# A written order for the experts' phase: 889 named steps in one list, in place of loops and a planner

## Chip, cores and metric

One core of one Trainium2 chip. The time is device microseconds (us) of one execution. A core has a matrix engine (PE, TensorE), three engines for elementwise work (DVE is VectorE, ACT is ScalarE, POOL is GpSimd), and SP (SyncE), which here only issues transfers (DMAs). Each engine takes its instructions in the order in which the program has them for that engine, and waits at an instruction until what it needs is there. So what a kernel decides, beside the work itself, is five orders.

## What is computed

The reference chains three layers. The first is attention with a window of 128 positions, the second a gated layer with a spatial mix; the change touches neither. The third, which the code calls the experts' part, is this:

```python
B, S, D = x.shape            # 4, 576, 512
E, Hd, K = 4, 64, 2          # experts, head size, experts kept for a position
logits = x @ w_gate
topk = np.argpartition(-logits, K, axis=-1)[..., :K]
w = softmax(logits[topk])
for e in range(E):
    q, k, v = x @ wq[e], x @ wk[e], x @ wv[e]
    scores = scale * (q @ k.transpose(0, 2, 1))
    scores = np.where(causal, -1e9, scores)
    a = softmax(scores)
    ye = a @ v @ wo[e]
    out += (gate of e at the position, 0 if e is not kept) * ye
```

The four experts are four heads of causal attention. Their gates are folded into the softmax's row factors, so that the four outputs add up in one product with `wo`.

## The kernel before

**Tiling.** A batch `b` (0 to 3) has 576 positions: four tiles of 128 queries (`j` = 0 to 3) and one of 64 (`j` = 4, in which two heads share the 128 rows). A tile sees the keys up to its own last position, so tile 0 has 128 keys a row and tile 3 has 512. Products of 32-bit data are made in three passes (`PASSES`): high by high, high by low, low by high part; a result in PSUM is therefore always taken in two steps, the high part by ACT (a copy), the low part by DVE (a subtraction, `lo_part`).

**The steps of a batch.** `load_g` fetches the batch's input from DRAM (`g_dram`) and splits it. `proj` makes queries and keys: 8 banks of 12 matmuls (tile `pq`: pair of heads, query or key, half of the positions), then the values (`values`, tile `pvB`, 12 matmuls each) and the gates (`gates`, 14 small operations on DVE, POOL and ACT). For each tile `scores_b` makes the scores of both pairs of heads (`psB`); `row_items` subtracts the row's maximum (DVE, one fused operation that also reduces) and takes the exponential (ACT); `weigh` makes the row factors (DVE) and scales (POOL). The weights must then be turned round for the next product. DVE turns blocks of 32 by 32 in place, and SP writes the tile to DRAM (`mid`, four DMAs) and reads it back in another order (`pTB`): `cross_items` and `read_back`. The last three tiles (`y, a, z`) are turned on PE instead (`turn_b`, tile `ptB`). `attend_b` multiplies by the values (`pxB`), `take_b` takes the result (`o`), `out_tile` multiplies by `wo` (`pout`), copies (`ot`) and stores.

**Buffers.** Four PSUM banks (`D`) serve `pq`, `pvB`, `pxB` and `pout` in turn; two double banks (`S`) serve `psB` and `ptB`. There are three buffers for a tile's weights (`pB`), three for the turned ones (`pTB`), three in DRAM (`mid`), two for a batch's queries, keys and values. A tile's DVE operation on the scores (L1168) therefore waits until the write of the tile three before it has landed.

**What sets the order.** Two ways are in use. The attention and gated layers follow long written lists of named steps (`OPENING`, `FIRST`, `SECOND`). The experts' phase does not: a loop over the 20 tiles places the PE's work, with `pull` interleaving projections and outputs between the scores and `attend_b` of a tile four places back (`LAG`), and the class `Flow` places the other engines' work from costs in ns written beside each operation (`item`) and from the PE time that it counts along. An operation goes to its engine's program when, by these costs, the PE has come that far:

```python
def pump(self):
    ...
    engine, ns, op, after, ok = items[0]
    at = max(chain[2], self.free.get(engine, 0.0))
    if at > self.pe or (ok and not ok()):
        break
```

A tile's write and read stand in one chain, with a pause between them that is taken from a table by `j`; a projection's 12 matmuls, or an output's 6, go into one bank, and the next bank is begun when they are done.

Of the kernel before, what the change touches and what calls it, by code (L numbers as in the profile page):

```python
# [10 lines left out]
F32 = mybir.dt.float32  # L11
# [12 lines left out]
P = 128  # L24
DM = 512
# [158 lines left out]
class Flow:  # L184


    def __init__(self):
        self.pe = 0.0
        self.free = {}
        self.chains = []  # L190
        self.count = 0

    def add(self, items, rank=1, delay=0.0, then=None):
        self.count += 1
        chain = [rank, self.count, self.pe + delay, deque(items), then]
        self.chains.append(chain)
        self.chains.sort(key=lambda c: c[:2])
        return chain

    def pump(self):  # L200
        moved = True
        while moved:
            moved = False
            for chain in list(self.chains):
                items = chain[3]
                while items:
                    engine, ns, op, after, ok = items[0]
                    at = max(chain[2], self.free.get(engine, 0.0))
                    if at > self.pe or (ok and not ok()):
                        break  # L210
                    items.popleft()
                    op()
                    self.free[engine] = at + ns
                    chain[2] = at + ns + after
                    moved = True
                if not items and chain in self.chains:
                    self.chains.remove(chain)
                    if chain[4]:
                        chain[4](chain[2])
                    moved = True  # L220
                    break

    def coming(self):
        return min((max(c[2], self.free.get(c[3][0][0], 0.0)) for c in self.chains if c[3] and (not c[3][0][4] or c[3][0][4]())), default=1e12)

    def work(self, ns):
        end = self.pe + ns
        self.pump()
        while (at := self.coming()) <= end:
            self.pe = max(self.pe, at)  # L230
            self.pump()
        self.pe = end

    def until(self, done):
        self.pump()
        while not done():
            self.pe = max(self.pe, self.coming())
            self.pump()

    def finish(self, chain):  # L240
        self.until(lambda: chain not in self.chains)


def item(engine, ns, op, after=0.0, ok=None):
    return engine, ns, op, after, ok
# [3 lines left out]
def block_kernel(ctx, tc, qP, kP, v, w_in, wspT, bsp, w_outT, wcat, wo, relt, tri, out):  # L249
# [683 lines left out]
    both = []  # L933

    def load_g(b, pool):
        G = x if b % 2 == 0 else x2
        f = pool.tile([P, 4, S], F32, tag="gf", name=f"gf{b}", bufs=1)

        def fetch(k, after=0.0):
            return "SP", 400.0, lambda: nc.sync.dma_start(f[:, k, :], g_dram[b, k]), after, None  # L940

        def parts():
            first = 2 if b > 1 else 4
            for k in range(first):
                yield fetch(k, 6000.0 if k == first - 1 else 0.0)
            for k in range(4):
                yield "ACT", 670.0, lambda k=k: nc.scalar.copy(G[0][:, k, :S], f[:, k, :]), 0.0, None
                on, ns, engine = ("DVE", 850.0, nc.vector) if b < 2 else ("POOL", 1430.0, nc.gpsimd)
                yield on, ns, lambda k=k, engine=engine: lo_part(G[1][:, k, :S], f[:, k, :], G[0][:, k, :S], engine), 2000.0 if b > 1 and 0 < k < 3 else 0.0, None
                if k + first < 4:  # L950
                    yield fetch(k + first)
            c = slice(64 * (b % 2), 64 * (b % 2) + 64)

            def high():
                if b % 2 == 0:
                    both[:] = [gfp.tile([P, 4, P], F32R, tag=f"both{i}", name=f"both{b}_{i}") for i in range(2)]
                nc.scalar.copy(both[0][:, :, c], f[:, :, 0:64])

            yield "ACT", 400.0, high, 0.0, lambda: tails_done[0] >= b // 2
            yield "POOL", 740.0, lambda: lo_part(both[1][:, :, c], f[:, :, 0:64], both[0][:, :, c], nc.gpsimd), 0.0, None  # L960

        return G, list(parts())

    tails_done = [0]
    G, gparts = load_g(0, gfp)
    for part in gparts:
        part[2]()
# [17 lines left out]
    QS, KS, QT, VS, GATE = {}, {}, {}, {}, {}  # L985

    flow = Flow()
    banks = []

    def bank(name):  # L990
        if len(banks) >= 4:
            flow.finish(banks[-4])
        banks.append(None)
        return len(banks) - 1, psD.tile([P, 512], F32, tag="D", name=name)

    def leave(n, *items, delay=250.0):
        banks[n] = flow.add(items, rank=0, delay=delay)
        return banks[n]

    gating = []  # L1000

    def gates(b, t0, n, after=()):
        if len(gating) > 1:
            flow.finish(gating[-2])
        vt = VS[b]
        lg = vt[:, t0 : t0 + n, 256:260]
# [24 lines left out]
        gating.append(flow.add([item(e, 230.0, op) for e, op in steps] + list(after)))
        gated[b, t0] = gating[-1]

    gated = {}

    def tail_gate(b):
        gt, gq = GATE[b]
        for o in range(2):
            yield item("ACT", 200.0, lambda o=o: nc.scalar.copy(gq[64 * o : 64 * o + 64, :], gt[0:64, 4, :].rearrange("p (r o) -> p o r", o=2)[:, o, :]))

    def values(b, t, stationary):
        at, pv = bank(f"pvB{b}_{t}")
        n = 0
        for i, j in PASSES:
            for k in range(4):
                nc.tensor.matmul(pv[:, :260], stationary(i, k), W[j][1][:, k, 512 - CUT :], start=(n == 0), stop=(n == 11))  # L1046
                n += 1
            if n < 12:
                yield 4 * 120.0
        if t < 4:  # L1050
            vt = VS[b]
            leave(at, item("ACT", 370.0, lambda: nc.scalar.copy(vt[:, t, :], pv[:, :260])))
        else:
            leave(at, *(item("ACT", 370.0, lambda o=o, vt=VS[b - 1 + o]: nc.scalar.copy(vt[:64, 4, :], pv[64 * o : 64 * o + 64, :260])) for o in range(2)))
        yield 4 * 120.0
        return at

    def proj(b, G):

        GATE[b] = wk.tile([P, 5, E], F32, tag="gt", name=f"gt{b}"), wk.tile([P, 2], F32, tag="gq", name=f"gq{b}")  # L1060
# [5 lines left out]
        for pr in range(2):  # L1066
            for role in (1, 0):
                hl = [t[:, pr, :] for t in (KS[b] if role else QS[b])]
                c0 = role * 256 + pr * 128
                for s in range(2):  # L1070
# [3 lines left out]
                    for i, j in PASSES:  # L1074
# [3 lines left out]
                        if n < 12:  # L1078
                            yield 4 * 133.0
# [22 lines left out]
        for chain in projected[b]:  # L1102
            flow.finish(chain)
# [399 lines left out]
```

## Time and profile before

| | us |
|---|---|
| median of 3 runs (450.99 to 451.58) | 451.36 |
| the profiled execution, its own time | 454.39 |
| its span, first to last instruction | 452.3 |
| PE busy in the span | 425.8 |
| DVE, ACT, POOL busy | 308.7, 239.2, 150.5 |
| PE's first matmul of the experts' phase | 268.03 |
| its last one starts at 447.52 and ends at about | 449.2 |

The rows further down come from the profiled execution; times in them count from the span's start. A busy PE is not PE at its best: matmuls overlap, their ends are modelled, and a matmul at half clock is busy for longer. Time in which an engine other than PE idles costs nothing by itself.

### The profile page before, as it was taken

Reading aid. Unit: us, or ns where it says so; the run is one execution under the profiler, and the core shown is the slowest. Engines: PE = TensorE matmul, PEld = TensorE weight load, DVE = VectorE, ACT = ScalarE, POOL = GpSimd, SP = SyncE. Lnnn points to the kernel's source line nnn. Section 1 sums busy time; section 2 is a strip of 40 time slices with the busy share of each in tenths; the row PEclk is TensorE's granted clock in tenths of the full one; section 3 lists DMA queues with packets and bytes.
Section 4 is the critical chain, followed back from the end, with each engine's and each line's share of the span. In section 5 each row is a group of like instructions: output and inputs, shape, how many; then the busy total and the mean of one; then the engine's idle time right before and its main releaser. Section 6 shows DMA issues by size and latency. Waiting matters only on the chain.

```text
span 452.3 us, 11412 instructions
## 1 busy us (share of the span) xinstructions
PE 425.8 (94%) x4055; PEld 378.4 (84%) x4055; DVE 308.7 (68%) x1062; ACT 239.2 (53%) x746; POOL 150.5 (33%) x281
## 2 busy tenths in 40 slices
PE   7888999999999999999999999999968989999786
PEld 6566799899898989899989999989957978887564
DVE  5999999989988656872464235377765675776331
ACT  6977879644645544551351134467454444564541
POOL 2064433263344520443000002357644442341200
PEclk9999999999999999999999999999998999999899
DMA  8986674687947644234674200136976575697863
GB/s 260 337 313 238 173 219 123 209 276 219 270 144 234 171 112 120 63 77 128 210 280 157 100 1 0 54 93 170 268 217 190 150 182 171 170 207 239 205 232 94
DMA packets 76940, 80.01 MB, mean 177 GB/s; under 512 B 18002, under 2 KB 52946, under 8 KB 76500
## 3 DMA queue, kind: packets, MB, share of 16 engines
q1 hardware_dynamic: 76740, 79.15, 59.2%
q8 instruction: 32, 0.52, 0.5%
q14 instruction: 24, 0.20, 0.2%
q10 hardware_dynamic: 144, 0.13, 0.1%
HBM read 49.64 MB, written 29.62 MB: 175 GB/s over the span
## 4 chain that ended last, share of the span: by engine, by line
PE 61%; DMA 15%; DVE 15%; SPq 3%; ACT 2%; issue 2%; POOL 2%; DVEq 0%; POOLq 0%; ACTq 0%
PE pg L763 12%; PE pu L748 11%; PE pv L685 9%; DMA pTB<-mid 8%; DMA mid<-pB 6%; PE pq L1076 6%; PE px L659 5%; PE pw L915 4%; DVE pB L1216 3%; PE pxB L1288 3%; SPq L1218 3%; PE pvB L1046 2%; PE pg L766 2%; DVE p L298 2%; POOL pB L311 1%
## 5 line engine op out<-in xcount | busy, mean ns | idle before, releaser
L299 ACT ACTIVATE p<-p,st 128x128 f32<-128x128 f32 x144 | 56.3, 394 | 12.1 <-DVE st L298 6.7
L763 PE MATMUL pg<-wsp,vn 128*128 128x288 f32 x384 | 60.2, 296 | 1.0 <-ACT vn L720 1.0
L748 PE MATMUL pu<-x,win 128*128 128x288 f32 x384 | 57.5, 296 | 0.0
L763 PEld LDWEIGHTS pg<-wsp,vn 128*128 128x128 f32 x384 | 54.3, 188 | 3.3 <-ACT vn L720 1.2
L685 PE MATMUL pv<-win,x 128*128 128x512 f32 x216 | 56.1, 398 | 0.0
L1076 PE MATMUL pq<-x,W 128*128 128x288 f32 x384 | 55.0, 301 | 0.0
L748 PEld LDWEIGHTS pu<-x,win 128*128 128x128 f32 x384 | 53.4, 188 | 1.8 <-issue 0.9
L1076 PEld LDWEIGHTS pq<-x,W 128*128 128x128 f32 x384 | 52.1, 191 | 1.9 <-issue 1.5
L311 POOL TENSOR_SCALAR pB<-pB,stB 128x384 f32<-128x384 f32 (+4 forms) x64 | 35.8, 575 | 36.4 <-DVE stB L1192 27.6
L578 POOL TENSOR_TENSOR p<-p,st 128x512 f32<-128x512 f32 (+1 forms) x28 | 29.6, 1058 | 55.0 <-ACT p L299 24.6
L685 PEld LDWEIGHTS pv<-win,x 128*128 128x128 f32 x216 | 38.6, 188 | 8.0 <-issue 1.1
L1169 ACT ACTIVATE pB<-pB,stB 128x128 f32<-128x128 f32 (+3 forms) x64 | 35.8, 560 | 15.3 <-DVE stB L1168 13.7
L1288 PE MATMUL pxB<-pTB,vt 128*64 128x128 f32 (+2 forms) x480 | 28.9, 266 | 8.8 <-DMA pTB<-mid 8.7
L1288 PEld LDWEIGHTS pxB<-pTB,vt 128*64 128x64 f32 (+1 forms) x480 | 23.6, 140 | 14.0 <-DMA pTB<-mid 5.7
L1216 DVE STREAM_TRANSPOSE pB<-pB 128x1024 f32<-128x1024 f32 (+3 forms) x28 | 27.0, 984 | 9.4 <-POOL pB L311 9.2
L1168 DVE CUSTOM_DVE_ANT_0 pB<-psB,trit 128x128 f32<-128x128 f32 (+3 forms) x64 | 28.5, 480 | 5.4 <-DMA mid<-pB 5.2
L298 DVE CUSTOM_DVE_ANT_0 p<-ps,relm 128x128 f32<-128x128 f32 x128 | 30.1, 284 | 0.3
L613 POOL TENSOR_SCALAR_AFFINE_SELECT pU<-pT 128x512 f32<-128x512 f32 (+1 forms) x26 | 15.8, 619 | 38.5 <-DMA pT<-carry 37.8
L1330 PE MATMUL pout<-wo,o 128*128 128x512 f32 x102 | 27.3, 412 | 0.8 <-ACT o L1301 0.8
L771 DVE TENSOR_TENSOR g<-u,pg 128x288 f32<-128x288 f32 x32 | 14.4, 450 | 19.7 <-PE pg L766 19.5
L299 ACT ACTIVATION_READ_ACCUMULATOR p<-p,st 128x1 f32 x144 | 27.3, 190 | 0.0
L659 PE MATMUL px<-pU,v 128*64 128x128 f32 (+1 forms) x256 | 23.6, 266 | 1.4 <-DVE st L575 1.1
(183 smaller groups left out, 897.1 us busy)
## 6 DMA issues: line engine op xcount, KB each, us to landing
carry<-p SPq DMA_DIRECT2D x96, 64.0 KB, 2.0
pT<-carry SPq DMA_DIRECT2D x24, 256.0 KB, 2.9
q<-in_qP SPq DMA_DIRECT2D x20, 256.0 KB, 3.6
g_dram<-g SPq DMA_DIRECT2D x16, 288.0 KB, 2.9
gf<-g_dram SPq DMA_DIRECT2D x16, 288.0 KB, 5.6
raw<-in_w_in SPq DMA_DIRECT2D x8, 512.0 KB, 5.9
v<-in_v SPq DMA_DIRECT2D x16, 256.0 KB, 5.3
mid<-pB SPq DMA_DIRECT2D x16, 256.0 KB, 4.8
```

The source lines that it names most:

```text
L298: lambda: nc.vector.tensor_tensor_reduce(s_view, ps_view, tab, -0.125, FLT_MAX, ALU.add, ALU.min, nm),
L299: lambda: nc.scalar.activation(s_view, s_view, AF.Exp, bias=nm, scale=-1.0, accum_out=sm),
L311: nc.gpsimd.tensor_scalar(p, p, r, 0.0, op0=ALU.mult, op1=ALU.add)
L578: ops["m"] = lambda: nc.gpsimd.tensor_tensor(blocks, blocks, sm.unsqueeze(1).unsqueeze(3).to_broadcast([P, 4, n, 32]), op=ALU.mult)
L659: nc.tensor.matmul(px[64 * o : 64 * o + 64, hp, :qn], V_[b, t][:, h * 64 : h * 64 + 64], rhs, start=(t == max(0, j - 1)), stop=(t == j))
L685: nc.tensor.matmul(pv, x[i][:, k, t0 : t0 + P], win[j][:, k, 512:1024], start=(n == 0 and k == 0), stop=(n == 2 and k == 3))
L748: nc.tensor.matmul(pu[:, :HALF], win[i][:, k, m * P : (m + 1) * P], x[j][:, k, c], start=(n == 0 and k == 0), stop=(n == 2 and k == 3))
L763: nc.tensor.matmul(pg[:, :HALF], vn[i][k][:, m * P : (m + 1) * P], wsp[j][:, k, c], start=(n == 0 and k == 0), stop=False)
L1076: nc.tensor.matmul(pq[:, :HALF], W[i][c0 // CUT][:, k, c0 % CUT : c0 % CUT + P], G[j][:, k, c], start=(n == 0), stop=(n == 11))
L1169: item("ACT", 480.0 + 0.84 * kn, lambda: nc.scalar.activation(part(p, i), part(p, i), AF.Exp, bias=nm, scale=-1.0, accum_out=sm)),
L1216: items.append(item("DVE", 130.0 + 1.12 * (c1 - c0), lambda flat=flat: nc.vector.transpose(flat, flat)))
L1288: nc.tensor.matmul(px[64 * o : 64 * o + 64, pr, :qn], vt[:kb, c, (2 * pr + o) * 64 : (2 * pr + o) * 64 + 64], rhs(pr, c, o), start=(c == 0 ...
```

## The change

The loop, the class `Flow`, `item`, and the costs go. In their place stands `THIRD`, one list of 889 names, each of them one step; `act` looks a name up and issues its instructions. All five engines' programs follow from that one list. The matmuls are the same ones, 1,482 of them in the phase, and so are the operations of the other engines; their places differ.

Names: `L`, `GH`, `GL`, `BH`, `BL` load and split an input; `Q` is a third of a projection bank (4 matmuls), `qh` and `ql` take it; `V`, `vr` the same for values; `g` one of the gate's 14 operations; `S` the scores of one pair of heads; `l`, `e`, `f`, `m`, `T` the row operations of a tile; `w` its four writes, `R` its read; `A` its product with the values, `oh` and `ol` take it; `O` a third of an output (2 matmuls), `oc` copies, `o` stores; `t`, `c` turn a tile on PE.

```diff
-class Flow:
...
+THIRD = """
+    L1.0 L1.1 L1.2 L1.3 Q0.1.0.1.0 VZ0 VZ1 Z0 Q0.0.0.0.0 Z1 Q0.0.0.0.1 Q0.1.0.1.1 Q0.1.0.1.2 Q0.0.0.0.2 V0.2.0 qh0.1.0.1 qh0.0.0.0 V0.0.0 ql0.1.0.1
...
+    m3.0.1 m3.0.2 m3.0.3 A2.4 oh3.3 R3.4 ol3.3 O3.3.0 oh2.4 O3.2.0 ol2.4 O3.1.0 O3.3.1 O3.1.1 O3.3.2 O3.2.1 oc3.3 O3.2.2 O3.1.2 o3.3 oc3.2 t3.0.0
...
+TURNED = ((3, 2), (3, 1), (3, 0))
...
+    def project(b, pr, role, s, n):
+        pq = bank("pq", b, pr, role, s)
+        G, c0, c = inputs(b), role * 256 + pr * 128, slice(s * HALF, (s + 1) * HALF)
+        i, j = PASSES[n]
+        for k in range(4):
+            nc.tensor.matmul(pq[:, :HALF], W[i][c0 // CUT][:, k, c0 % CUT : c0 % CUT + P], G[j][:, k, c], start=(n == k == 0), stop=(n == 2 and k == 3))
...
+    def scores_b(b, j, pr):
+        q0, kn = TOK[j][0], keys_seen(j)
+        Q, K = heads(b, 0), heads(b, 1)
+        view = score_bank(b, j, pr)
...
+    def send(b, j):
+        p = weights(b, j)[0]
+        n, w, e = sizes(j)
+        mid = get(("mid", b, j), lambda: dram.tile([16 if j < 4 else 18, 32, 4, w], F32, tag=f"mid{w}", name=f"mid{b}_{j}", bufs=3))
+        for q in range(4):
             nc.sync.dma_start(mid[:n, :, q, :].rearrange("k i w -> i k w"), p[32 * q : 32 * q + 32, : n * w].rearrange("i (k w) -> i k w", w=w))
...
+    def out_tile(b, t, n, h=None):
+        c = slice(0, DM) if h is None else slice(256 * h, 256 * h + 256)
+        po = bank("pout", b, t, h)
+        o2 = made["o", b if t < 4 else b - 1, t]
+        i, j = PASSES[n]
+        for pr in range(2):
+            nc.tensor.matmul(po[:, : c.stop - c.start], o2[i][:, pr, :], wos[j][:, pr, c], start=(n == pr == 0), stop=(n == 2 and pr == 1))
...
+        else:
+            {"Q": project, "sp": spread, "V": value, "vr": value_take, "h": tail_gate, "S": scores_b, "l": row_min, "e": row_exp, "f": factors, "m": scale, "T": turn_blocks,
+             "w": send, "R": read_back, "t": turn_b, "c": turn_take, "A": attend_b, "oc": out_take, "o": out_store}[kind](*key)
...
-    todo = deque([proj(0, G)])
-    credit = [0.0]
...
-    for s in range(len(tiles) - 1):
-        b, j = tiles[s]
...
-        scores_b(*tiles[s])
-        due = tiles[s - LAG] if s >= LAG else None
-        for i in range(5):
-            if due and (state[due]["read"] or i == 2):
-                close_tile(due)
-                due = None
-            pull((5500.0 if s < 1 else RATE if s < 15 else 4600.0 if s < 18 else 2000.0) / 5)
...
+    for name in THIRD.split():
+        act(name)
```

**SP, around the writes of tiles (0, 3) and (0, 4).** `mid0_3` is the DRAM copy of tile (0, 3), `pTB0_3` its read, `gf3` a load of batch 3's input. Before:

```order
L1218 DMA mid0_3_4423<-pB0_3_4305 32x16x128 x4
L1218 DMA mid0_4_4495<-pB0_4_4394 32x18x64 x4
L1235 DMA pTB0_3_4666<-mid0_3_4423 128x4x512
L940 DMA gf3_4508<-g_dram_84 128x576
L1218 DMA mid1_0_4641<-pB1_0_4510 32x4x128 x4
L940 DMA gf3_4508<-g_dram_84 128x576
L1235 DMA pTB1_0_4756<-mid1_0_4641 128x512
L1235 DMA pTB0_4_4760<-mid0_4_4495 128x4x256
L1235 DMA pTB0_4_4760<-mid0_4_4495 64x256
```

And now:

```order
L1146 DMA mid0_4_4529<-pB0_4_4323 32x18x64 x4
L1146 DMA mid0_3_4575<-pB0_3_4373 32x16x128 x4
L930 DMA gf3_4419<-g_dram_84 128x576
L1156 DMA pTB0_4_4653<-mid0_4_4529 128x4x256
L1156 DMA pTB0_4_4653<-mid0_4_4529 64x256
L1146 DMA mid1_0_4716<-pB1_0_4495 32x4x128 x4
L1156 DMA pTB0_3_4752<-mid0_3_4575 128x4x512
L930 DMA gf3_4419<-g_dram_84 128x576
```

Tile (0, 4) is now written before (0, 3), and its read stands ahead of the write of (1, 0) where it stood behind that write and the read that waits for it.

**PE, around the product of tile (0, 3) with its values** (`pxB0_3`; `psB1_3` are scores of batch 1, `pq2` and `pq3` projections of batches 2 and 3, `pvB2` values of batch 2). Before:

```order
L1076 MATMUL pq2_1_1_1_4763<-x0_104,W0_388_3383 128x288 x4
L1076 MATMUL pq2_1_1_1_4763<-x1_105,W0_388_3383 128x288 x4
L1076 MATMUL pq2_1_1_1_4763<-x0_104,W1_388_3385 128x288 x4
L1288 MATMUL pxB0_3_4781<-pTB0_3_4666,vt0_3969 64x128 x16
L1076 MATMUL pq2_1_0_0_4810<-x0_104,W0_384_3382 128x288 x4
L1076 MATMUL pq2_1_0_0_4810<-x1_105,W0_384_3382 128x288 x4
L1076 MATMUL pq2_1_0_0_4810<-x0_104,W1_384_3384 128x288 x4
L1076 MATMUL pq2_1_0_1_4830<-x0_104,W0_384_3382 128x288 x4
```

And now:

```order
L1083 MATMUL psB1_3_1_4856<-k1_0_4103,q1_0_4088 128x512 x2
L1083 MATMUL psB1_3_1_4856<-k1_1_4104,q1_0_4088 128x512 x2
L1083 MATMUL psB1_3_1_4856<-k1_0_4103,q1_1_4089 128x512 x2
L1192 MATMUL pxB0_4_4868<-pTB0_4_4653,vt0_3834 64x64 x20
L1192 MATMUL pxB0_3_4892<-pTB0_3_4752,vt0_3834 64x128 x16
L1025 MATMUL pvB2_0_4918<-W0_388_3383,x0_104 128x260 x4
L1025 MATMUL pvB2_0_4918<-W1_388_3385,x0_104 128x260 x4
L1025 MATMUL pvB2_1_4945<-W0_388_3383,x0_104 128x260 x4
L1025 MATMUL pvB2_1_4945<-W1_388_3385,x0_104 128x260 x4
L1001 MATMUL pq3_0_0_1_4957<-x20_3811,W0_384_3382 128x288 x4
```

The product of (0, 3) now stands behind all projections of batch 2, all scores of batch 1 and the product of (0, 4), where it stood ahead of the last two.

**PE, the end** (`pout3_3` is the output of tile (3, 3), `ptB3_0` the turning of tile (3, 0)). Before:

```order
L1260 MATMUL ptB3_0_0_6055<-ident_74,pB3_0_5962 128x128 x4
L1330 MATMUL pout3_3_6061<-wo0_3801,o3_3_0_6048 128x512 x2
L1330 MATMUL pout3_3_6061<-wo1_3802,o3_3_0_6048 128x512 x2
L1330 MATMUL pout3_3_6061<-wo0_3801,o3_3_1_6049 128x512 x2
L1288 MATMUL pxB3_1_6071<-pTB3_1_0_6004,vt3_5410 64x128 x8
L1330 MATMUL pout3_1_6085<-wo0_3801,o3_1_0_6080 128x512 x2
L1330 MATMUL pout3_1_6085<-wo1_3802,o3_1_0_6080 128x512 x2
L1330 MATMUL pout3_1_6085<-wo0_3801,o3_1_1_6081 128x512 x2
L1288 MATMUL pxB3_4_6094<-pTB3_4_5919,vt3_5410 64x64 x20
L1330 MATMUL pout3_4_6118<-wo0_3801,o2_4_0_5907 128x512 x2
```

And now:

```order
L1192 MATMUL pxB2_4_6026<-pTB2_4_5786,vt2_4931 64x64 x20
L1210 MATMUL pout3_3_None_6054<-wo0_3801,o3_3_0_6047 128x512 x2
L1210 MATMUL pout3_2_None_6060<-wo0_3801,o3_2_0_5994 128x512 x2
L1210 MATMUL pout3_1_None_6064<-wo0_3801,o3_1_0_6018 128x512 x2
L1210 MATMUL pout3_3_None_6054<-wo1_3802,o3_3_0_6047 128x512 x2
L1210 MATMUL pout3_1_None_6064<-wo1_3802,o3_1_0_6018 128x512 x2
L1210 MATMUL pout3_3_None_6054<-wo0_3801,o3_3_1_6048 128x512 x2
L1210 MATMUL pout3_2_None_6060<-wo1_3802,o3_2_0_5994 128x512 x2
L1210 MATMUL pout3_2_None_6060<-wo0_3801,o3_2_1_5995 128x512 x2
L1210 MATMUL pout3_1_None_6064<-wo0_3801,o3_1_1_6019 128x512 x2
L1171 MATMUL ptB3_0_0_6084<-ident_74,pB3_0_5931 128x128 x4
L1192 MATMUL pxB3_4_6092<-pTB3_4_6050,vt3_5394 64x64 x20
```

Products stood alternating with the output that needs them; now three outputs are mixed in thirds and stand between the products of (2, 4) and (3, 4). In the order of SP, the read of (3, 4) is issued at `R3.4`, ahead of these nine thirds.

## Rows read from the trace of the kernel before

**Rows 1.** Windows: busy us of each engine by stage, clock, DMA share

```profile
core 0: us, PE busy (x) PEld busy (x) DVE busy (x) ACT busy (x) POOL busy (x), PEclk, DMA share, GB/s
60.00:220.00 160.00, 160.00 (x1691) 145.62 (x1684) 125.09 (x442) 82.80 (x287) 60.39 (x86) 1.00 0.56 164
...
268.00:300.00 32.00, 32.00 (x258) 31.07 (x257) 16.57 (x53) 15.98 (x45) 8.93 (x27) 1.00 0.16 44
...
328.00:345.00 17.00, 11.54 (x126) 9.47 (x124) 9.32 (x30) 7.92 (x25) 9.70 (x19) 0.97 0.72 209
...
268.00:449.30 181.30, 166.84 (x1483) 147.47 (x1481) 107.64 (x374) 91.48 (x270) 66.47 (x147) 0.98 0.60 163
449.30:452.30 3.00, 0.00 (x0) 0.00 (x0) 0.00 (x0) 0.35 (x1) 0.00 (x0) 1.00 0.34 102
```

**Rows 2.** Waits of PE from 268 us on: total, times, longest

```profile
PE pxB L1288 <- DMA pTB<-mid: 8.7, 6, 3.1
PE ptB L1260 <- DVE stB L1168: 2.7, 1, 2.7
PE pout L1330 <- ACT o L1301: 0.8, 2, 0.5
...
PE pout L1320 <- ACT o L1301: 0.5, 1, 0.5
```

**Rows 3.** Timeline of PE; brackets: idle before, and what ended it

```profile
303.61 1.66 PE L1138 MATMUL psB<-k,q 64*128 64x512 f32 x12
...
335.56 1.97 PE L1288 MATMUL pxB<-pTB,vt 128*64 128x128 f32 x32 [3.05 <-DMA pTB<-mid]
...
343.06 2.39 PE L1288 MATMUL pxB<-pTB,vt 128*64 128x64 f32 x40 [1.61 <-DMA pTB<-mid]
...
397.42 4.42 PE L1330 MATMUL pout<-wo,o 128*128 128x512 f32 x18
...
426.50 1.12 PE L1260 MATMUL ptB<-ident,pB 128*128 128x128 f32 x4 [2.69 <-DVE stB L1168]
```

**Rows 4.** Timeline of SP around the first long waits of PE

```profile
318.93 8.51 SPq L1218 DMA_DIRECT2D mid<-pB  x8
327.62 0.77 SPq L1235 DMA_DIRECT2D pTB<-mid  x1
...
337.16 1.92 SPq L1235 DMA_DIRECT2D pTB<-mid  x3
```

**Rows 5.** Windows of ten us: clock and transfers

```profile
320.00:330.00 10.00, 9.20 (x89) 8.29 (x87) 7.27 (x31) 5.52 (x21) 5.68 (x10) 1.00 0.99 255
...
340.00:350.00 10.00, 8.38 (x82) 7.43 (x81) 5.80 (x16) 3.64 (x11) 5.42 (x11) 0.83 0.69 191
...
420.00:430.00 10.00, 7.31 (x74) 5.72 (x72) 4.19 (x20) 4.75 (x15) 2.27 (x4) 0.83 0.87 194
```

**Rows 6.** Chain that ended last, in order of time: start, us, what

```profile
248.46 0.53 PE pg L763 x4
...
268.03 12.69 PE pq L1076 x96
280.72 5.74 PE pvB L1046 x48
...
294.21 3.88 PE pq L1076 x28
...
337.60 5.42 DMA pTB<-mid
...
376.10 4.11 DMA pTB<-mid
```

**Rows 7.** Waits of DVE from 268 us on

```profile
DVE pB L1168 <- DMA mid<-pB: 5.2, 2, 3.8
```

**Rows 8.** Window from the first read to the last ones

```profile
297.00:436.00 139.00, 125.94 (x1131) 110.04 (x1131) 90.86 (x322) 73.77 (x223) 57.74 (x121) 0.98 0.73 195
```

More of the change, by code (lines that the diff above doesn't have):

```diff
@@ L181, in drain @@
         self.credit = 0.0
-class Flow:
[L187 to L241, printed above, removed]
@@ L248, in block_kernel @@
+"""
+TURNED = ((3, 2), (3, 1), (3, 0))
 @with_exitstack
@@ L930, in block_kernel, with load_g @@
     dense.through("u3_1")
-    both = []
-    def load_g(b, pool):
+    gf_, both_ = {}, {}
+    def load_g(name):
+        kind, b, k = re.match(r"(L|GH|GL|BH|BL)(\d)(?:\.(\d))?$", name).groups()
+        b = int(b)
         G = x if b % 2 == 0 else x2
[L937 to L951, printed above, removed]
-            c = slice(64 * (b % 2), 64 * (b % 2) + 64)
[L954 to L962, printed above, removed]
@@ L1002, in gates, with get, bank, inputs @@
[L1002 to L1006, printed above, removed]
+    made = {}
+    def get(key, make):
+        if key not in made:
+            made[key] = make()
+        return made[key]
+    def bank(kind, *key):
+        return get((kind, *key), lambda: psD.tile([P, 512], F32, tag="D", name=kind + "_".join(map(str, key))))
+    def inputs(b):
+        return x if b % 2 == 0 else x2
+    def heads(b, role):
+        tag = "qk"[role]
+        return get((tag, b), lambda: [wk.tile([P, 2, S], F32R, tag=f"{tag}{i}", name=f"{tag}{b}_{i}") for i in range(2)])
@@ new lines, in value, with value_take @@
+    def value(b, t, n):
+        pv = bank("pvB", b, t)
+        i, j = PASSES[n]
+        for k in range(4):
+            if t < 4:
+                rows = inputs(b)[i][:, k, COL[t] : COL[t] + P]
+            else:
+                rows = both_[b // 2][i][:, k, :]
+            nc.tensor.matmul(pv[:, :260], rows, W[j][1][:, k, 512 - CUT :], start=(n == k == 0), stop=(n == 2 and k == 3))
+    def value_take(b, t):
+        pv = bank("pvB", b, t)
+        if t < 4:
+            nc.scalar.copy(values(b)[:, t, :], pv[:, :260])
+        else:
+            for o in range(2):
+                nc.scalar.copy(values(b - 1 + o)[:64, 4, :], pv[64 * o : 64 * o + 64, :260])
@@ L1036, in tail_gate @@
     def tail_gate(b):
-        gt, gq = GATE[b]
+        gt, gq = gate_of(b)
         for o in range(2):
[L1039 to L1052, printed above, removed]
-        else:
-            leave(at, *(item("ACT", 370.0, lambda o=o, vt=VS[b - 1 + o]: nc.scalar.copy(vt[:64, 4, :], pv[64 * o : 64 * o + 64, :260])) for o in range(2)))
-        yield 4 * 120.0
-        return at
@@ L1232, in read_back @@
+    ready = {}
+    def read_back(b, j):
+        n, w, e = sizes(j)
+        mid = made["mid", b, j]
         pT = wk.tile([P, 16 * P], F32, tag="pT", name=f"pTB{b}_{j}", bufs=3)
@@ L1281, in attend_b @@
[L1281 to L1283 removed]
+        px = bank("pxB", b, j).rearrange("p (r c) -> p r c", r=4)
+        vt, rhs = values(b), ready[b, j]
         for pr in range(2):
[L1285 removed]
+            for c in range(j + 1):
                 kb = 64 if c == 4 else 128
```

561 lines of the change are left out of this document (221 added, 340 removed).

## The prediction, made before the changed kernel was run

> **What bounds the kernel now.** I read the windows by stage first [rows 1]. Between 60 and 220 us the two earlier layers keep PE busy for 160 of 160 us, so nothing in an order can be gained there as long as the matmuls are the same. The experts' phase is otherwise: from 268.0 to 449.3 us PE is busy for 166.8 of 181.3 us, so it waits for 14.5 us. The first 32 us of the phase have no wait; the stage from 328 to 345 us has 5.5 us of it. Behind the last matmul come 3.0 us (a copy and a store).
>
> Then the list of PE's waits [rows 2]: 8.7 us for turned weights to land (`pTB<-mid`), 2.7 us once for DVE to finish weights that PE is to turn, and 1.3 us at the end, 0.8 + 0.5, for ACT's copy of a product. These make 12.7 of the 14.5 us. The timeline shows where: 3.05 us ahead of the product of tile (0, 3), 1.61 us ahead of (0, 4), 2.69 us at 426.5 us [rows 3]. SP's timeline says why the first two come together [rows 4]: the eight writes of (0, 3) and (0, 4) take from 318.93 to 327.4 us to issue; the first read is issued at 327.62 us, and the reads of (0, 4) only at 337.16 us, because in SP's order they stand behind the writes of the next batch's tile 0 and behind that tile's read, which has to wait. PE's product of (0, 3) starts at 335.56 us, 30.3 us after its scores ended (303.61 + 1.66).
>
> Last, the clock [rows 5]. In the ten us from 340 and again from 420 the granted mean is 0.83, elsewhere 1.0 apart from small dips: PE ran there for a while at the lower of its two levels, 1.2 GHz instead of 2.4, right behind the waits of rows 3. A mean of 0.83 over 10 us is 1.7 us of full clock lost, 3.4 us for both. These hide in the busy time.
>
> So the phase is limited by PE, with 14.5 us of waits and 3.4 us of slow clock on top. Those 17.9 us are what an order can win, and little more.
>
> **The change, part by part.**
>
> *The same work.* The matmuls are the same, and so are DVE's 107.6, ACT's 91.5 and POOL's 66.5 us in the 181.3 us [rows 1]. In a phase of 165 us they would be 65, 55 and 40% busy. None becomes the bound by its amount.
>
> *Thirds in place of whole banks.* Projections, values and outputs are now interleaved in groups of 4 or 2 matmuls. That could cost something at each change of bank, of which there are 138 more (207 groups for 69 banks). From above: the price of a change between kinds of matmul, which comes next, 0.09 us each, gives 12 us. From below, nothing: in the gated layer, which is already written in thirds, a group of four 288-column matmuls between other groups takes 0.53 us, 132 ns each, and 96 projection matmuls in one stretch take 12.69 us, also 132 ns [rows 6]. That is the same shape, so I take nothing.
>
> *Pairs scored apart.* Scores use half of the array's rows, products with values half of its columns (64*128 and 128*64 in rows 3), the rest all of it. 28 projection matmuls between two scorings take 3.88 us, and at 132 ns they would take 3.70 [rows 6]: 0.18 us for two changes, 0.09 each. Counted in the PE's order, the phase has 62 stretches of one kind before and 44 after, since products and scorings now stand side by side more often. 18 changes fewer save 1.6 us; the bounds are 0 and that.
>
> The Trainium skill speaks against this part: "TensorEngine Tiling (Array Packing)", Key Properties, says that changing the tiling mode drains the engine. The 0.18 us of the row agrees that it costs something; how many changes there are is for the order to say (rival E).
>
> *Landings.* Of the order I take what stands on PE between the place that starts a wait and the place that ends it, at the prices of the rows, as the lead. For (0, 3), between its last scores and its product stand 26 projection thirds and 8 value thirds, 17.6 us by rows 6, and four products and ten scorings of a pair, 11.5 us by their sizes (the largest product 1.97 us, the largest scoring half of 1.66 [rows 3]): 29.1 us, where before it took 30.3 us with SP's detour. I take the 1.2 us that are lacking as a wait; (0, 4) now is read before the next batch's write and has 29.7 us, 13 of them after its read. The other tiles of batches 0 to 2 have 24 to 42 us. The closest read is the last, (3, 4): between `R3.4` and `A3.4` stand nine output thirds and four transposes. 18 output matmuls take 4.42 us [rows 3], the transposes about 0.6 (half of the 1.12 us that four took in the slow slice), so 5.0 us; reads of the same shape took 5.42 and 4.11 us [rows 6]. I take 0.4 us, bounds 0 and 2.
>
> *Weights' buffers.* DVE's work on a tile's scores waits until the tile three before is written; this happened twice, 5.2 us, the longest 3.8 [rows 7]. From the issue of a write to that place the new list leaves 5.3 us (smallest tile) to 12.6 of PE work. The worst case in the trace is (0, 3), 8.7 us from first write to read [rows 4], and it has 8.8. I take nothing; the bound is in the rivals.
>
> *PE turning.* The tile that was waited for (2.69 us) now has 13 us of other work between its scores and its turning, and the two after it 6 and 17. I take the wait as gone.
>
> *The end.* The last products still feed outputs through an ACT copy. Three thirds of other outputs or a product now cover most of it, but I leave the whole 1.3 us in.
>
> *The clock.* Both falls came behind waits of about 3 us or of two near each other. With no wait above 1.2 us left I count both as gone: 3.4 us. From below, nothing gained.
>
> The sum, against the profiled execution: 452.3 − 14.5 − 3.4 − 1.6 + (1.2 + 0.4 + 1.3) = 435.7 us of span, 16.6 us less. The execution itself took 454.39 us, 2.1 more than its span, and the median of the runs is 451.36; I take the 16.6 us from the median: **434.8 us**.
>
> **The rivals.**
>
> *A. The landings stay late.* The leads are PE work, and a shorter phase moves the same bytes faster. From 297 to 436 us the transfers ran at 195 GB/s [rows 8], 27.1 MB; in 129 us this asks for 210. In the fullest stretch they moved 255 GB/s at a share of 0.99 [rows 5], and there the first wait followed. For it: (0, 3), (3, 4) and several buffers have margins of a us or less, and one late read in a list with a fixed order holds all five engines. Against it: writes come evenly in the list, one or two in each 10 us. If the 8.7 us of rows 2 stay instead of 1.6, and one fall of the clock (1.7): 434.8 + 7.1 + 1.7 = 443.6 us.
>
> *B. DVE stands at the buffers (slower).* Behind a DVE operation that waits for a write stand the low parts of projections, which the next scores need and which free PE's banks; some of these banks have about 1.0 us until they are wanted again. So each such wait shows on PE nearly whole. There are 16 such places; at the mean of the two seen, 2.6 us, seven of them make 18.2 us: 434.8 + 18.2 = 453.0 us. From 16.6 us on, that is from the seventh, the change loses. Against it: only two in the order of before, and now leads at or above the longest seen.
>
> *C. Transfers set the end, and the change does nothing.* If 195 GB/s were all there is, 27.1 MB from 297 us on would end at 436 us as before, and so would the kernel: 451 us. The 255 GB/s of rows 5 speak against it.
>
> *D. Better than forecast.* No waits at all, the 2.9 us gone too: 431.9 us.
>
> *E. Every pair pays for itself.* If each of the 16 half-array scorings, now two, cost its two changes more, that is 32 changes at 0.09 us, 2.9 us, in place of the 1.6 saved: 439.3 us. The count of 44 stretches speaks against it.
>
> **How the numbers follow.** The forecast, with D as its lower edge, 431 to 438.5 us: 0.65. A: 0.24, B: 0.05, C: 0.04, E: 0.02. About 0.2% (0.9 us) is what a measurement of this kernel can tell from no change. Forecast, A and E are all faster: 0.91; C is the same to within that, 0.04; B slower, 0.05. The range for 8 in 10 takes the forecast and A: from 430.9, one us under D, to 444.0. The likeliest case's own is 431.5 to 438.5.
>
> **What would show it.** Right: from 268 us on PE idles for 2 to 5 us in place of 14.5, no wait for `pTB<-mid` above 1.5 us, no slice at 0.83, the last matmul at about 433 us, the stage before 268 us as it was. The thirds are wrong if PE is busy throughout and the phase still takes over 168 us. A shows as waits of PE for `pTB<-mid` near (0, 3), (1, 3) or (3, 4), with a slow slice behind them; B as waits of DVE's score operation (L1168 before) for `mid<-pB` with idle PE just behind; C as a DMA share near 1 all through. What I would have missed altogether is a wait that comes only from the list: an operation placed ahead of one that PE needs sooner, on ACT or POOL, of which the trace of before says nothing.

## The result, and the profile after

Four runs of the changed kernel took 435.32 us in the median (434.60 to 435.67), four of the kernel before 451.18 (450.08 to 451.58): a ratio of 0.965, interval 0.9629 to 0.9672, so 15.9 us less. The forecast was 434.8. The profiled execution took 435.67 us, with a span of 433.6.

The windows by stage, with the columns of [rows 1]: the earlier layers, the phase up to about a microsecond behind its last matmul, the stage that held 5.5 us of waits, and the two stretches where the clock had fallen [rows 5].

```profile
60.00:220.00 160.00, 159.72 (x1679) 145.44 (x1678) 122.78 (x438) 82.70 (x285) 61.86 (x85) 1.00 0.56 163
268.00:430.60 162.60, 160.89 (x1484) 145.90 (x1482) 108.29 (x374) 92.74 (x270) 65.88 (x143) 1.00 0.66 181
328.00:345.00 17.00, 17.00 (x185) 15.69 (x182) 13.87 (x47) 10.25 (x30) 11.39 (x23) 1.00 0.73 217
340.00:350.00 10.00, 10.00 (x99) 9.83 (x96) 6.59 (x19) 5.32 (x15) 5.30 (x8) 1.00 0.74 169
420.00:430.00 10.00, 9.64 (x87) 7.82 (x85) 1.30 (x4) 3.66 (x8) 0.00 (x0) 1.00 0.29 105
```

The stage before 268 us is as it was. DVE, ACT and POOL are busy for the same time as in [rows 1], to 1.3 us. PE is busy for 160.9 us and idles for 1.7, of which about 0.95 lies behind its last matmul. The mean clock is 1.00 throughout. Of all the waits of [rows 2] none is left. This is the whole list of PE's waits after 268 us, then the only waiting row of its timeline, and the products of (0, 4) and (0, 3) and of (3, 4), each without a bracket:

```profile
PE psB L1083 <- DVE stB L1104: 0.7, 1, 0.7
```

```profile
292.04 0.62 PE L1083 MATMUL psB<-k,q 64*128 64x256 f32 x6 [0.74 <-DVE stB L1104]
...
338.00 3.17 PE L1192 MATMUL pxB<-pTB,vt 128*64 128x64 f32 x62
...
424.23 2.41 PE L1192 MATMUL pxB<-pTB,vt 128*64 128x64 f32 x48
```

SP's timeline answers [rows 4]: the reads of (0, 4) are issued at 324.75 us, some 12 us sooner than before; that of (0, 3) at 329.22, which is 1.6 us later, but its product also comes later, at about 339.8 us, where PE had wanted it at 332.5.

```profile
316.60 7.04 SPq L1146 DMA_DIRECT2D mid<-pB  x8
323.69 0.89 SPq L930 DMA_DIRECT2D gf<-g_dram  x1
324.75 1.56 SPq L1156 DMA_DIRECT2D pTB<-mid  x2
327.36 1.76 SPq L1146 DMA_DIRECT2D mid<-pB  x4
329.22 0.39 SPq L1156 DMA_DIRECT2D pTB<-mid  x1
```

The end has grown. The last matmul ends at about 429.65 us, 4.0 us ahead of the span's end, where it was 3.0 [rows 1]:

```profile
428.06 1.58 PE L1210 MATMUL pout<-wo,o 128*128 128x256 f32 x12
...
428.92 1.13 SPq L1229 DMA_DIRECT2D out<-ot  x2
...
429.72 0.37 ACT L1218 COPY ot<-pout 128x256 f32<-128x256 f32 x1 [0.83 <-PE pout L1210]
430.12 0.39 ACTq L1224 DMA_DIRECT2D out<-ot  x1
430.14 0.54 SPq L1224 DMA_DIRECT2D out<-ot  x1
```

### The profile page after: what moved, and what is told of

It is laid out like the page before. It is cut to its first block, busy times and chain, and to the rows that moved or that the text cites. A ratio compares the mean times of both kernels' runs of the same rounds, so it can differ in the third digit from the quotient of the medians.

```text
span 433.6 us, 11406 instructions
## 1 busy us (share of the span) xinstructions
PE 419.6 (97%) x4055; PEld 376.8 (87%) x4055; DVE 306.9 (71%) x1062; ACT 240.3 (55%) x746; POOL 152.8 (35%) x281
## 4 chain that ended last, share of the span: by engine, by line
PE 82%; DVE 10%; DMA 3%; ACT 3%; issue 1%; SPq 1%; DVEq 0%; ACTq 0%
PE pq L1001 12%; PE pg L750 11%; PE pu L735 11%; PE pv L672 8%; PE pvB L1025 6%; PE pxB L1192 6%; PE pout_None L1210 6%; PE px L646 5%; PE psB L1083 4%; PE pw L902 4%; DVE p L285 2%; PE psB L1088 2%; PE pg L753 2%; DMA carry<-p 2%; PE ps L529 1%
## 5 line engine op out<-in xcount | busy, mean ns | idle before, releaser
L1001 PE MATMUL pq<-x,W 128*128 128x288 f32 x384 | 57.1, 297 | 0.0
L1113 ACT ACTIVATE pB<-pB,stB 128x128 f32<-128x128 f32 (+4 forms) x72 | 41.8, 583 | 13.2 <-DVE stB L1104 4.8
L1025 PE MATMUL pvB<-W,x 128*128 128x260 f32 x192 | 27.4, 284 | 0.0
L1192 PE MATMUL pxB<-pTB,vt 128*64 128x128 f32 (+2 forms) x480 | 26.7, 261 | 0.0
L1210 PE MATMUL pout_None<-wo,o 128*128 128x512 f32 x102 | 26.4, 400 | 0.0
```

What stands on the lines that cost most here:

```text
L1001: nc.tensor.matmul(pq[:, :HALF], W[i][c0 // CUT][:, k, c0 % CUT : c0 % CUT + P], G[j][:, k, c], start=(n == k == 0), stop=(n == 2 and k == 3))
L1025: nc.tensor.matmul(pv[:, :260], rows, W[j][1][:, k, 512 - CUT :], start=(n == k == 0), stop=(n == 2 and k == 3))
L1113: nc.scalar.activation(part(i), part(i), AF.Exp, bias=st[:, i : i + 1], scale=-1.0, accum_out=st[:, 4 + i : 5 + i])
L1192: nc.tensor.matmul(px[64 * o : 64 * o + 64, pr, :qn], vt[:kb, c, (2 * pr + o) * 64 : (2 * pr + o) * 64 + 64], rhs(pr, c, o), start=(c == 0 ...
L1210: nc.tensor.matmul(po[:, : c.stop - c.start], o2[i][:, pr, :], wos[j][:, pr, c], start=(n == pr == 0), stop=(n == 2 and pr == 1))
```

## The experiments

Three sets of runs, each beside runs of the kernel before, whose medians were 451.19 (16 runs), 452.07 (17) and 451.71 us (9).

### Whole banks again: `whole_banks`

```diff
-V1.3.1 ... Q1.1.0.1.0 ... V1.3.2 S0.4.1 ... Q1.1.0.1.1 ... Q1.0.1.1.0 ... Q1.0.1.1.1 ... S0.3.0
+V1.3.0 V1.3.1 V1.3.2 S0.4.1 ... S0.3.0
```

> The changed kernel with the three thirds of every projection, value and output bank side by side again, at the place of the last third; all else in the written order as it is. If thirds cost nothing and the gain comes from where the landings and the products stand, this is within 1 us of the changed kernel (434.3 to 436.3 us). If the thirds themselves keep PE from waiting for banks, PE gets waits of 0.4 to 1 us at a good part of the 69 banks, 3 to 6 us in all (438 to 441 us).

It took 438.23 us (437.06 to 439.18), ratio 0.9701 (0.9661 to 0.9742): 2.9 us of the gain lost. That is the second outcome's time but not its mechanism: PE has no wait for the banks of the projections. Its waits grew to 2.9 us, three of them, all for a score bank; the longest stands ahead of the second pair of (0, 3):

```profile
307.68 1.31 PE L1081 MATMUL psB<-k,q 64*128 64x512 f32 x12 [1.91 <-DVE stB L1102]
```

and this is what DVE did until it gave the bank back at 307.5 us:

```profile
301.78 0.46 DVE L261 TENSOR_TENSOR k<-pq,k 128x288 fp32r<-128x288 f32 x1 [1.13 <-ACT k L1005]
...
304.45 1.82 DVE L1137 STREAM_TRANSPOSE pB<-pB 128x768 f32<-128x768 f32 x2
...
306.24 0.67 DVE L1102 CUSTOM_DVE_ANT_0 pB<-psB,trit 128x512 f32<-128x512 f32 x1
306.85 0.07 DVE L1102 DVE_READ_ACCUMULATOR2_ANT stB<- 128x1 f32 x1
306.85 0.68 DVE L1102 CUSTOM_DVE_ANT_0 pB<-psB,trit 128x512 f32<-128x512 f32 x1
```

DVE's order is the same in both kernels. In the changed one it gives this bank back at 309.0 us, later still, but PE gets there only at 309.56: seven thirds stand between the scorings `S0.3.1` and `S0.3.0`, here three. So the thirds do more than cost nothing. They are the fill between scorings. The clock has a part in the loss, too: its mean is 0.97 in the ten us from 300 and 0.86 in those from 310, 1.7 us of full clock in this execution.

### Whole banks at the first third's place: `whole_first`

```diff
-S0.3.1 ... V1.0.0 ... V1.3.1 ... S0.4.1 ... Q1.0.1.1.0 ... Q1.0.1.1.1 ... S0.3.0
+S0.3.1 ... V1.0.0 V1.0.1 V1.0.2 ... S0.4.1 ... Q1.0.1.1.0 Q1.0.1.1.1 Q1.0.1.1.2 ... S0.3.0
```

> The changed kernel with the three passes of every projection, value and output bank side by side at the FIRST one's place (whole_banks had them at the last one's); 44 stretches of one kind, as in the changed kernel. Theory (thirds between the scorings give VectorE time to free score banks; without them TensorE comes to a score before its bank is free, wherever the whole bank stands): 1 to 4 us of waits for score banks, 436.5 to 439.5. Rival (whole_banks lost only because its banks began later and so ended late for ScalarE's and VectorE's copies: VectorE stood 1.13 us for a copy of k at 301.8): here every bank ends sooner than in the changed kernel, no such wait, 434.8 to 435.9.

It took 437.18 us (436.93 to 438.23), ratio 0.9676 (0.965 to 0.9701). The time is in the theory's range, but not for its reason: no wait for a score bank was added, so whole banks do not bring those waits wherever they stand. Nor is it the rival's 434.8 to 435.9. Here nine thirds stand between `S0.3.1` and `S0.3.0`, and that is enough. Beside the changed kernel's one wait two others came:

```profile
PE psB L1082 <- DVE stB L1103: 0.7, 1, 0.7
PE pvB L1024 <- ACT vt L1029: 0.7, 1, 0.7
PE ptB L1170 <- DVE pB L1126: 0.6, 1, 0.6
```

and PE was busy for 161.9 us, 1.0 more, at a clock of 0.999. The two waits make 1.3 us, the busy time 1.0. Of this, 0.3 us only say that the phase began at 268.38 us, not at 268.05; what the other 0.7 are, no row here names. The profiled execution, 438.23 us, is the longest of five; by the medians the loss is 1.5 us beside the changed kernel in the same set (435.69, below), 1.9 beside 435.32.

### Pairs of scores together: `pairs_together`

```diff
-S0.3.1 l0.4.0 g0.4.9
+S0.3.1 S0.3.0 l0.4.0 g0.4.9
```

> The changed kernel with the scores of both pairs of a tile side by side again, at the place of the first. 40 stretches of one kind of matmul in place of 44. If the landings made the gain, this costs only waits for the second double bank, as before (two waits of 0.8 us there): 0 to 3 us more, 435 to 438 us. If scoring pairs apart is a main part of the gain, PE waits before most of the 12 tiles that need two double banks, and the time is 441 us or more.

It took 438.35 us (437.94 to 441.07), ratio 0.9722 (0.9682 to 0.9761): 3.0 us lost, at 40 stretches of one kind in place of 44. The waits are the same in kind, the longest again at (0, 3):

```profile
306.50 0.96 PE L1081 MATMUL psB<-k,q 64*128 64x512 f32 x6 [2.27 <-DVE stB L1102]
```

Four changes between kinds fewer did not pay for 3.3 us of new waits. Behind the 2.27 us the clock did not fall: its mean is 1.00 in the twenty us from 300.

### Both undone: `coarse`

```diff
-S0.4.1 ... S0.3.1 ... V1.0.0 ... V1.3.1 ... S0.3.0 ... S1.0.0
+S0.4.1 ... S0.3.1 S0.3.0 ... V1.3.0 V1.3.1 V1.3.2 ... S1.0.0
```

> The changed kernel with both splittings undone: the three passes of every projection and output side by side, and both pairs of a score side by side; what is left of the change is the written order with its earlier reads. If what the two give is separate, their costs add (2.9 and 3.0 us over 435.3): about 441.2, 440 to 442.5, and TensorE waits 4 to 6 us for score banks. If one place of wait is shared by both, 438 to 439.5. If each covers for the other, 443 and more.

It took 444.64 us (442.82 to 445.13), ratio 0.9841 (0.9812 to 0.9869): 9.3 us more than 435.32 (8.9 more than `tail`, below, in the same set), where the two alone lost 5.9 together. So each covers for the other, the third of the outcomes that were named, and the written order without either split keeps only 7.4 us of the gain. What waits is the score banks, not a landing:

```profile
PE psB L1081 <- DVE stB L1102: 5.6, 5, 3.1
PE ptB L1169 <- DVE stB L1106: 1.1, 2, 0.9
PE psB L1081 <- DVE sm L1056: 0.7, 1, 0.7
```

The longest, 3.08 us, stands ahead of the same `S0.3.0`, between which and `S0.3.1` no third is left. A clock fall came with it:

```profile
300.00:310.00 10.00, 6.92 (x49) 5.72 (x47) 7.80 (x25) 2.58 (x7) 7.22 (x18) 0.87 0.68 168
310.00:320.00 10.00, 10.00 (x69) 9.65 (x70) 3.37 (x12) 5.42 (x16) 3.18 (x5) 0.79 0.60 181
```

PE's clock means 0.87 and 0.79 in these 20 us: 3.4 us of full clock, about 3.0 of them while PE was busy, on top of the waits. The list was written for the splits; what another list with whole banks and whole scorings would give was not tried.

### The price of a change between kinds: `interleaved`, `fewer`

In `interleaved` the half-array scorings are mixed, pass by pass, with a projection or value third, so that the same matmuls make 102 stretches in place of 44:

```diff
+        other = partner(at) if name[0] == "S" and name[3] != "4" else None
...
+            between[:] = [lambda k=k: part(other, [k]) for k in range(2)]
+            act(name)
+            part(other, [2, 3])
```

> The changed kernel with the matmuls of half-array scorings mixed with those of a projection or value third (two, one, two, one, two, two): 102 stretches of one kind where the changed kernel has 44, the same matmuls. If a change between kinds costs 0.09 us as read from one stretch of before, 58 more cost 5.2 us: about 440.5 us. If it costs nothing, and the 0.18 us of that stretch were something else, 435 to 436 us. If the array empties at each, 0.2 us or more a change: 447 us or more.

It took 447.79 us (445.78 to 449.29), ratio 0.9914 (0.9885 to 0.9943), with the one wait of 0.7 us that the changed kernel has too. In the profiled execution, 446.55 us, the clock is 1.00 up to the last matmul (the row's 0.99 takes in the time behind it). From 268 us to its end PE was busy for 171.74 us:

```profile
268.00:460.00 192.00, 171.74 (x1483) 148.53 (x1481) 108.15 (x374) 92.00 (x270) 65.88 (x143) 0.99 0.58 156
```

That is 10.85 us more than the 160.89 above, for 58 changes more: 0.19 us each, twice the 0.09 that I took from one stretch of 28 matmuls [rows 6]. The Trainium skill ("TensorEngine Tiling (Array Packing)", Key Properties) says that changing the tiling mode drains the engine. The trace agrees that a change costs time, 0.19 us here; that it is a drain, no row shows.

`fewer` goes the other way: two items moved, 41 stretches.

```diff
-Q3.0.0.0.0 oh1.1 m2.0.2 R1.3 m2.0.3 ol1.1 S2.3.0
+oh1.1 m2.0.2 R1.3 m2.0.3 ol1.1 S2.3.0 Q3.0.0.0.0
...
-S0.2.0 e0.1.1
+S0.2.0 S0.2.1 e0.1.1
```

> The changed kernel with two items moved: the second pair of scores of (0,2) right behind the first, and one projection pass that stood alone between products and scores of image 1 and 2 moved behind those scores; 41 stretches for 44, nothing else. Theory (each change between kinds costs 0.14 to 0.19 us and no engine is late there): 0.4 to 0.6 us less, 434.7 to 435.2, if no wait for a score bank comes instead. Rival (the split pair is what keeps the score banks free, in this place too): a new wait of 0.5 to 2 us, 435.5 to 437.

It took 435.23 us (434.03 to 435.38), ratio 0.9628 (0.9604 to 0.9652), beside 435.69 for the changed kernel in the same set, with no new wait. In the windows from 268 us on PE was busy for 160.62 us against 160.96, but the phase does not begin at the same time in the two. These are its first and last matmuls in `fewer`, then in the changed kernel:

```profile
268.32 1.88 PE L999 MATMUL pq<-x,W 128*128 128x288 f32 x13
...
427.78 1.58 PE L1208 MATMUL pout<-wo,o 128*128 128x256 f32 x12
```

```profile
268.10 2.15 PE L1001 MATMUL pq<-x,W 128*128 128x288 f32 x15
...
428.12 1.58 PE L1210 MATMUL pout<-wo,o 128*128 128x256 f32 x12
```

So the phase takes 161.04 us against 161.60, 0.56 less, or 0.19 us for each of three changes, the price that `interleaved` gave. In the first trace of the changed kernel and in `tail`, which have the same order of PE, it takes 161.59 both times. By the time of the whole kernel, `fewer` has the fastest median of the study and beats the kernel before, but the changed kernel by less than can be told: the two intervals overlap.

### A read later, a read sooner: `late_read`, `read_sooner`

```diff
-l1.2.0 R0.3 m1.1.2 ... R1.0 ql2.1.1.0
+l1.2.0 m1.1.2 ... R1.0 R0.3 ql2.1.1.0
```

> The changed kernel with one name moved: the read of tile (0, 3) stands behind the read of (1, 0) in SP's order, the kind of place that the read of (0, 4) had before. The read is then issued some 6 us later, at about 335.5 us, and lands at about 343.5; its product is wanted at 339.9 us. If landings against leads are what PE waits for, PE waits there for 3 to 5 us, the clock falls behind it, and the time is 438.5 to 441 us. If reads have slack in the new list, or the later matmuls take it up, less than 1 us more.

It took 438.54 us (436.72 to 438.61), ratio 0.9702 (0.9658 to 0.9747). The wait came, at the product that wants the read, though shorter than the 3 to 5 us expected:

```profile
340.81 1.97 PE L1190 MATMUL pxB<-pTB,vt 128*64 128x128 f32 x32 [1.83 <-DMA pTB<-mid]
```

The profiled execution is the quickest of four, 436.72 us at a clock of 1.000. Its span is only 1.0 us longer than the changed kernel's (434.6 against 433.6), but its phase began 0.84 us sooner, at 267.21 us in place of 268.05. From the first projection to the end of the last matmul it takes 163.5 us against 161.6: the later matmuls take up nothing, and the wait costs its full length. The other three took 438.5 to 438.6 at a clock of 0.996, with spans of 436.4 and 436.5, 2.8 to 2.9 us longer.

`read_sooner` does the reverse in the kernel before. In its table of pauses the read-back of a tile 4 comes sooner, and nothing else differs. In SP's order this puts the reads of (0, 4) and (1, 4) ahead of those of (1, 0) and (2, 0):

```diff
-(1900.0, 3500.0, 3500.0, 5100.0, 6200.0)[j]
+(1900.0, 3500.0, 3500.0, 5100.0, 4000.0)[j]
```

> The kernel before with one number changed: SP takes the read-back of the weights of (0,4) (image 0, the tail rows) and its few neighbours earlier in its order; TensorE's, VectorE's, ScalarE's and GpSimd's orders stand as they were. Theory (the waits come from where SP's order puts a read): the 1.61 us wait ahead of the product of (0,4) goes and the clock fall behind it (1.7 us by half of the two falls) goes with it or not: 1.6 to 3.7 us off 451.2, 447.5 to 449.6, and the wait of 1.6 is absent from the list of TensorE's waits. Rival (the reads are late because the transfers are slow, not because of their place): the wait stays within 0.5 us of 1.6 and the time within 0.9 of 451.2.

It took 451.26 us (448.79 to 454.22, 12 runs), ratio 0.999 (0.9958 to 1.0022): nothing that can be told, and not the 447.5 to 449.6 of the theory, though the wait of 1.61 us is gone. Landings did get better and something else worse. Here are the three largest groups of PE's waits:

```profile
PE ptB L1260 <- DVE stB L1168: 3.7, 1, 3.7
PE pxB L1288 <- DVE pB L1216: 2.5, 1, 2.5
PE pxB L1288 <- DMA pTB<-mid: 1.7, 2, 0.9
```

The landings fell from 8.7 us [rows 2] to 1.7, or 4.2 with the row above them, which is the product of (0, 3) under another releaser. A part of this is chance: in the second trace of the unchanged kernel, below, they are 4.3, or 6.9 with the like row, and the 1.61 us are absent there, too. But the turning at the end now waits for 3.7 us in place of 2.7 (2.5 in the second trace), because DVE, ahead of it, stands longer at the buffers of [rows 7]:

```profile
DVE pB L1168 <- DMA mid<-pB: 6.2, 2, 4.7
```

So the two reads moved alone hand some of their gain, 1.0 to 1.2 us, on to the next late thing. All waits of PE add up to 11.6 us, against 14.2 and 13.9 in the two traces before; whether that is a gain in time the medians do not tell.

### Both kernels once more: `before_again`, `after_again`

> The kernel before once more, unchanged, for a second trace of it: if the waits of TensorE behind 268 us are a property of the order, their sum comes out within 1.5 us of the 14.5 of the first trace, and the three largest (about 3.05, 2.69 and 1.61) stand at the same operations. If they are chance, sum and places differ. The span of the first, 452.3, is expected to be high by 1 to 3 us, with the excess in the clock falls.

Its execution took 455.3 us, span 453.2, clock 0.988. PE's waits add up to 13.9 us by the list, against 14.2 in the first trace, and the waits of about 2.5 us ahead of (0, 3) and of the turning are there again. The 1.61 us ahead of (0, 4) are not, and the list puts the wait ahead of (0, 3) down to another releaser:

```profile
335.04 2.47 PE L1288 MATMUL pxB<-pTB,vt 128*64 128x128 f32 x32 [2.55 <-DVE pB L1216]
...
342.38 1.82 PE L1288 MATMUL pxB<-pTB,vt 128*64 128x64 f32 x40
```

Three ten-us windows, not two, have a mean clock of 0.83. So sum and main places belong to the order; the smaller waits and the number of clock falls change from run to run. That the first trace's span is long by chance, as I expected, this does not settle: the second is longer still.

> The changed kernel once more, unchanged, beside the other two on the same chip. If its time is free of waits that change from run to run: 434.5 to 436, a spread of at most 1.5 us (the kernel before spreads over 5), and one wait of TensorE of 0.7 us, at the same place. Otherwise the list of waits has other places and the spread is 3 us or more.

It took 435.69 us (435.03 to 435.80), ratio 0.9641 (0.9618 to 0.9664), with the one wait of 0.74 us at the same place. Both kernels' times in all the sets: 434.6 to 435.8 after (9 runs), 449.0 to 455.3 before.

### The end: `tail`

```diff
-                nc.sync.dma_start(out[b - 1 + i, t0:S, :], ot[64 * i : 64 * i + 64])
+                (nc.sync, nc.scalar if b == 3 else nc.sync)[i].dma_start(out[b - 1 + i, t0:S, :], ot[64 * i : 64 * i + 64])
```

> The changed kernel, with the second of the two stores of the last tail rows issued by ScalarE's queue instead of SP's. Theory (the last store on SP, 0.54 us from 430.14, only starts there because the two stores ahead of it take 1.13 us from 428.92): SP's last store starts near 429.5, the end is set by ScalarE's store at about 430.1, and the span's end comes 0.6 to 0.9 us after-wards less: 3.9 to 4.0 us from the last matmul to the end become 3.0 to 3.4, the time 434.4 to 434.8 against 435.3. Rival (the last landing costs the same wherever it is issued): within 0.3 us of 435.3.

It took 435.75 us (434.66 to 436.39), ratio 0.965 (0.9624 to 0.9676): no gain, and 0.4 us above 435.3, so in neither of the ranges named; the changed kernel's own runs reach 435.80. SP's last store does go out 0.8 us sooner:

```profile
429.34 0.54 SPq L1224 DMA_DIRECT2D out<-ot  x1
429.51 0.37 ACT L1218 COPY ot<-pout 128x256 f32<-128x256 f32 x1 [0.78 <-PE pout L1210]
429.91 0.36 ACTq L1224 DMA_DIRECT2D out<-ot  x1
```

But its last matmul ends at 429.47 us and the span at 433.2, still 3.7 us later (4.0 in the changed kernel; 3.0 to 3.4 were expected). A store on ACT's queue now takes 2.7 us to land, in the median of two, where it took 2.2 in the changed kernel and 1.7 before. SP's queue was not what held the end. That the stores of (3, 4), issued 2.5 us ahead of the last one before and 1.2 us now, land together with it fits these landings, but was not tried.

## Why the prediction was right, and where it was off

*Waits gone: right, by the mechanism given.* Landings, turning and the ends for which I kept 2.9 us do not wait at all. That the leads did it, `late_read` shows for one read: put back, it brings a wait of 1.8 us, and the phase is 1.9 us longer. For the other reads and the turning it rests on the list of waits.

*The waits that I kept: wrong ones.* None of the three came. For (0, 3) the lead was right, about 29 us from its scores to its product, but I held it against the 30.3 us of before; the read is issued at 329.22 us and lands 6.4 us later, at 335.6, which is 25 us behind the scores and 4 us ahead of the product. For (3, 4) the read goes out at 417.31 us and lands 5.0 us later, 1.9 us ahead of its product at 424.23. One wait of 0.74 us came for a score bank, a kind that I gave no term. Measured against forecast: 0.74 instead of 2.9. So two of the signs that I named for being right are missing: PE does not idle for 2 to 5 us, and its last matmul does not stand at about 433 us.

*The clock: right.* No slice at 0.83, 3.4 us back. `coarse` shows a fall right behind a wait of 3.1 us, `whole_banks` one behind 1.9. The length of a wait does not decide it alone: behind 2.27 us in `pairs_together` and 1.83 us in the trace of `late_read` the clock stayed at 1.00.

*Changes between kinds: right in sign, the price half of what it is.* Forecast 1.6 us for 18 fewer, at 0.09 each. Put in finely they cost 0.19 each, three taken out gave 0.19 each. The 0.18 us that I read from one row and divided by two are the size of one change. Without the waits and the clock PE was busy for 163.4 us before (166.8 − 3.4) and 160.9 now: 2.5 us, 0.14 for each of 18. That all of the 2.5 are changes is not shown: `whole_banks`, `pairs_together` and `coarse` have 41, 40 and 38 stretches, and their PE, counted from the first projection and without waits and clock falls, is busy for 160.7 us each, against 160.8 for the changed kernel. At 0.19 us a change they should have 0.6 to 1.1 us less, so something else costs time there, or the price is not the same in every place.

*Thirds at nothing: right as a cost, wrong as a whole.* I looked for a cost of splitting and found none, and the runs with whole banks show none: there PE is no less busy (160.7 us in `whole_banks`, 161.6 in `whole_first`, counted as above, against 160.8). The price of not splitting I did not look for. Without thirds 2.9 us are lost, or 1.5 to 1.9 with the whole banks at the first third's place; without scoring pairs apart 3.0, without both 9.3. The list of waits before had 0.8 + 0.7 us for score banks:

```profile
PE psB L1138 <- DVE stB L1168: 0.8, 1, 0.8
PE psB L1138 <- DVE stB L1173: 0.7, 1, 0.7
```

I took them as small change, though in the new order they are what comes next.

*Rivals.* A (late landings) did not come; the 240 GB/s that were moved from 360 to 410 us did not hold a read up. B did not come: DVE has no wait for a weights' buffer left. C is refuted by the time, E by the count of stretches and by the busy time. D, no waits, is the nearest in PE's part: its last matmul ends at 429.65 us, where the forecast's sum had 432.7.

*The end.* I left the 3.0 us behind the last matmul as they were. They are 4.0.

*From the span to the median.* The sum said 435.7 us of span and it is 433.6: 2.1 less (2.2 from waits, 0.9 from PE's busy time, −0.95 from the end). Yet the median is 0.5 above the forecast. The step that failed is the one that took 16.6 us, worked out on an execution of 454.39 us, from a median of 451.36. 18.7 us of span went, but 3.0 of these only brought that long execution down to its median. Two errors of 2 to 3 us nearly cancelled, so that the forecast came within 0.5 us is in part luck.

## What to carry to other kernels

A split that costs nothing can still be worth something: ask which engine's result the finer pieces give time to, and count the work between two uses of one buffer, as here between two scorings. Moving one late transfer in an order where several things are late can hand a part of its gain on to the next, as 1.0 to 1.2 us did here. Compare a phase from its own first instruction: here it began between 267.0 and 268.4 us, and windows from a fixed time hid up to 0.8 us by that. And a gain worked out on one profiled execution holds for that execution: where runs of the kernel before spread over 6 us, first take off what its own waits and clock falls have above the median.

## What the runs showed of the hardware that was not expected

A change between half-array and whole-array matmuls cost 0.19 us, both where 58 were put in among single matmuls and where three were taken out. The clock fell behind a wait of PE of 1.9 us (`whole_banks`) and did not behind one of 2.27 (`pairs_together`); what decides it stays open. Four executions of `late_read` differ by 1.9 us, three at a mean clock of 0.996 and one at 1.000; only the one at 1.000 has a trace, so where the clock fell in the others is not seen.
